# A planner's margin behind DMA loads: readers of fresh transfers placed later unless they are urgent

## The chip, the cores and the metric

The kernel runs on one core of one Trainium2 chip. The metric is device time in microseconds of one execution, as the median of several timed runs. Beside these, one execution is taken with the hardware profiler; all views of the profile come from it.

## The reference

A Mamba2-like scan over 4 sequences of 768 tokens (8 heads, head size 32, state size 16) feeds a mixture of four ReLU experts. Cut to what matters:

```python
# attention: x (4,8,768,32), a (4,8,768), B and C (4,8,768,16), float32
for c in range(nc):
    cum = np.cumsum(log_a[:, :, sl], axis=-1)
    L = np.exp(cum[:, :, :, None] - cum[:, :, None, :]) * causal
    M = np.einsum('bhin,bhjn->bhij', Cc, Bc) * L
    y[:, :, sl] = einsum(M, xc) + einsum(Cc, state) * np.exp(cum)[..., None]
    state = decay_full * state + np.sum(Bx * decay_from_j, axis=2)
x = y.transpose(0, 2, 1, 3).reshape(3072, 256)
# experts: w1 (4,256,1024), w2 (4,1024,256), domain_probs (3072,4)
p = domain_probs / (domain_probs.sum(-1, keepdims=True) + 1e-9)
for e in range(4):
    out += p[:, e:e+1] * (np.maximum(x @ w1[e], 0.0) @ w2[e])
```

## The kernel before

The 3,072 tokens are cut into 24 chunks of 128, and these into four blocks of six chunks (three pairs each; `ORDER = H, H, H, H`). The experts' hidden units are cut into 16 columns of 256. Within a block the two matrix products of the experts are done for three columns at a time with a bilinear scheme, which takes 15 block products where the plain way takes 18, at the price of sums of weights (L958), of tokens (L977) and of results (L896, L1178). One block product is `product` (L869): two matmuls of 128x128 by 128x256 in float32, four records in the profile. Sums of weights are made once, in the first block, stored to device memory (L963) and loaded again by later blocks (L955).

The attention of a chunk goes like this. `fetch` (L739) loads the chunk's tokens and B, C (`xb`, L430 to L434), the decays spread over the partitions (`ab`, L437) and those by head (`ah`, L443). `decays` makes the masks of decays with a scan on VectorE (L493, reads `ab`), the masked C on ScalarE (`mask`, L469: two multiplications of 128x128, `ctm` from `xb`), the faded B on GpSimd (`fade`, L503, reads `xb`), the decay factors (`dec`, L775, reads `ah`) and their product `cts` on GpSimd (L778). `scores` (L476) multiplies on TensorE, VectorE masks the result (L793), `outputs` (L815, L509) forms the chunk's result and `carry` (L846) the state.

None of the engines' orders after the start is written out by hand. `Plan` collects pieces of work with what each reads and writes, and with the engines that can do it and a cost in microseconds for each; some sums can go to VectorE or to GpSimd. The order of TensorE is a fixed list, `line`. `Plan.times` goes through it and gives each piece of work a time `latest`, the last start that does not make TensorE wait. `Plan.run` then walks an event clock: at each step it takes the engine that is free first, looks at its open pieces of work, finds for each when its inputs are there and its tile is free, and starts the one with the smallest `latest` among those that can start. A piece of work that isn't ready is passed over. At the end all work is issued in the order of planned starts, so each engine gets a fixed list of instructions and executes it in that order, waiting on semaphores.

All loads and stores of this part are issued from one queue, SP. The plan books a transfer with `kb` kilobytes as issue of .48 us a piece, 1.4 us, the bytes at 330 a microsecond one after another, and .7 us (L259 to L265). A reader on another engine that needs a transfer (`n.kb`) is taken as ready `MARGIN` = 2.0 us after the planned end; a reader of another engine's result as ready `HOP` = .06 us after it. `late` is how far TensorE is behind its list at that moment of the plan.

Of the kernel before, what the change touches and what calls it, by code (L numbers as in the profile page):

```python
# [18 lines left out]
HOP = 0.06  # L19
# [6 lines left out]
SOFT = 1  # L26
ROUND = 0, 4, 3, 2
RATE, MARGIN = 330.0, 2.0
AFTER = 1
HOLD = 6.0  # L30
NEAR, WORTH, FIRST = .3, 1.0, 25.0
# [45 lines left out]
class Plan:  # L77
# [105 lines left out]
    def run(self, line, at, begin):  # L183
# [19 lines left out]
        while todo:  # L203
            e = min(t, key=lambda e: t[e])
            now = t[e]
            best, soon, near = None, None, None
            late = self.late = max(0.0, t["PE"] - line[head].nominal) if head < len(line) else 0.0
            for w in waiting[e]:
                if w.start is not None or e == "PE" and w.place != head:
                    continue  # L210
                ready = max([w.ready, w.after.nominal + late if w.after else 0.0] + [
                    n.end + (MARGIN if n.kb and e != "SP" else -n.lag if n.by == e == "PE" else HOP)
                    for n in w.needs])
                if len(w.on) > 1 and e == "POOL":
                    if max(ready, now) + w.on[e] > w.latest + late + SLACK or self.backlog(
                            waiting["DVE"], now, t["DVE"], w) < (BACK if now > EASY else 99):
                        continue
                rank = w.latest
                if e == "DVE" and w.two and self.port > now + 0.05:
                    rank += YIELD  # L220
                if best is not None and ready <= now and rank >= best[0]:
                    continue
                when, homes = self.homed(
                    w, max(now, ready, self.port if e == "POOL" and w.port else 0.0))
                if when is None:
                    continue
                if when <= now + 0.02:
                    if best is None or rank < best[0]:
                        if e == "DVE" and w.two:
                            when = max(when, self.port)  # L230
                        best = rank, w, when, homes
                else:
                    if e == "DVE" and when <= now + NEAR and now < FIRST and (near is None or rank < near[0]):
                        near = rank, when
                    if soon is None or when < soon:
                        soon = when
# [16 lines left out]
            _, w, when, homes = best  # L253
# [86 lines left out]
def kernel(  # L340
# [882 lines left out]
    def leave(k, O, due):  # L1223
        for n in range(len(O)):
            o, ot = O[n], value("V")
            dve(D512, lambda e, o=o, ot=ot: nc.vector.transpose(flat(ot), flat(o)),
                reads=[o], writes=[ot])
            for c in (blocks[k].first + 2 * n, blocks[k].first + 2 * n + 1):
                dst = out[real(c) * P:real(c) * P + P].rearrange(
                    "(b i) (d a j) -> a d i b j", i=32, j=32, d=2)  # L1230
                for d in range(2):
                    for q in (0, 2):
                        def fn(e, c=c, d=d, q=q, dst=dst, ot=ot):
                            v = ot.t.rearrange("p d (b j) -> p d b j", j=32)
                            for x in (q, q + 1):
                                nc.sync.dma_start(
                                    out=dst[x, d],
                                    in_=v[32 * x:32 * x + 32, d, c % 2 * 4:c % 2 * 4 + 4])
                        dma(fn, 2, 150, reads=[ot], due=due)
# [105 lines left out]
    for u, (k, groups) in enumerate(units):  # L1345
# [20 lines left out]
        if ending is not None:  # L1366
            leave(*ending, due=lambda n=u + AFTER: ends[min(n, len(ends) - 1)])
            ending = None
# [90 lines left out]
```

## Time and profile before

| | |
|---|---|
| timed runs | 627.46, 628.15, 630.9 us; median 628.15 us |
| profiled execution, whole time | 2278.26 us |
| its span, first to last instruction | 2276.5 us |
| TensorE busy, matmul records | 2270.6 us, 3403 |
| VectorE busy | 566.9 us |
| ScalarE busy | 285.1 us |
| GpSimd busy | 132.8 us |
| moved by DMA | 99.51 MB, mean 44 GB/s |

The profiled execution is much longer than the timed runs. In the views, PE is TensorE's matmul, PEld its load of weights, DVE is VectorE, ACT is ScalarE, POOL is GpSimd and SP is the queue that issues the transfers. A line of a group has the source line, engine, operation, tiles and shapes, then busy time and mean duration in ns, then the idle time of the engine just ahead of it and what ended it. A line of waits has the engine and line that waited, what for, the total in us, how many times, and in the views of single engines the longest. A line of the timeline has the start, the duration in us, the instruction, and in brackets the idle time before it.

### The profile page before, as it was taken

What the parts mean: (1) busy time and instruction counts of PE and PEld (TensorE: products, weight loads), DVE (VectorE), ACT (ScalarE), POOL (GpSimd) and SP (SyncE); (2) the same over time, 40 slices, a digit from 0 to 9 for tenths busy, and PEclk for the clock granted to TensorE, in tenths of its full rate; (3) what the DMA queues carried; (4) which work ended last, traced back from release to release, by engine and by line L of the source; (5) the groups of instructions that cost most, each with busy time, mean ns of one, the idle gap of its engine ahead of it and who ended that gap; (6) DMA issues with size and microseconds to landing.
All of it is one profiled execution on the core that took longest, in us unless ns stands there. A gap on an engine that the chain in (4) does not pass through costs nothing.

```text
span 2276.5 us, 10010 instructions
## 1 busy us (share of the span) xinstructions
PE 2270.6 (100%) x3403; PEld 1200.0 (53%) x3403; DVE 566.9 (25%) x953; ACT 285.1 (13%) x597; POOL 132.8 (6%) x169
## 2 busy tenths in 40 slices
PE   9999999999999999999999999999999999999999
PEld 4555555555555555555555555555555555555555
DVE  3222222222222323222222231212212221212121
ACT  1000111111111111121110111101100011111100
POOL 1110101010121000000000000000000000000000
DMA  3311111111011212120011111101000211110000
GB/s 126 100 60 64 44 53 49 59 48 42 21 33 34 85 41 65 38 72 28 30 38 38 37 58 39 50 26 39 27 24 11 54 37 44 58 33 28 1 0 14
DMA packets 89203, 99.51 MB, mean 44 GB/s; under 512 B 27060, under 2 KB 62784, under 8 KB 89152
## 3 DMA queue, kind: packets, MB, share of 16 engines
q1 hardware_dynamic: 88996, 98.82, 13.9%
q8 instruction: 27, 0.44, 0.1%
q14 instruction: 24, 0.20, 0.0%
q10 hardware_dynamic: 156, 0.06, 0.0%
HBM read 82.34 MB, written 16.50 MB: 43 GB/s over the span
## 4 chain that ended last, share of the span: by engine, by line
PE 65%; ACT 0%; issue 0%
PE bank L869 64%; PE bank L509 1%; PE bank L476 1%; PE bank L815 0%; PE bank L1250 0%; ACT v L1255 0%; ACT v L830 0%; ACT A L519 0%
## 5 line engine op out<-in xcount | busy, mean ns | idle before, releaser
L869 PE MATMUL bank<-v,w 128*128 128x256 f32 x1780 | 1526.4, 1107 | 0.5 <-ACT v L830 0.5
L869 PEld LDWEIGHTS bank<-v,w 128*128 128x128 f32 x1780 | 773.0, 435 | 685.9 <-issue 671.2
L869 PE MATMUL bank<-Y,w 128*128 128x256 f32 x836 | 744.1, 1096 | 0.0
L869 PEld LDWEIGHTS bank<-Y,w 128*128 128x128 f32 x836 | 369.8, 442 | 316.4 <-issue 304.7
L904 DVE SCALAR_TENSOR_TENSOR v<-bank,gate 128x512 f32<-128x512 f32 x154 | 105.2, 689 | 681.7 <-PE bank L869 647.3
L896 DVE TENSOR_TENSOR v<-v,v 128x512 f32<-128x512 f32 x276 | 188.2, 716 | 84.0 <-ACT v L878 83.0
L896 DVE TENSOR_TENSOR v<-bank,v 128x512 f32<-128x512 f32 x76 | 52.6, 692 | 600.7 <-PE bank L869 596.1
L1127 ACT COPY v<-bank 128x512 f32<-128x512 f32 x140 | 82.1, 587 | 931.3 <-PE bank L869 931.3
L883 ACT COPY bank<-v 128x512 f32<-128x512 f32 (+1 forms) x222 | 124.4, 575 | 292.1 <-DVE v L896 210.5
L878 ACT COPY v<-bank 128x512 f32<-128x512 f32 x76 | 44.5, 586 | 493.4 <-PE bank L869 486.4
L896 POOL TENSOR_TENSOR v<-v,v 128x512 f32<-128x512 f32 x28 | 39.4, 1414 | 969.9 <-DVE v L896 553.0
L958 POOL TENSOR_TENSOR w<-w,w 128x256 f32<-128x256 f32 x48 | 36.9, 783 | 292.5 <-PE bank L869 232.3
L493 DVE TENSOR_TENSOR_SCAN LT<-ab,ident 128x512 f32<-128x512 f32 x42 | 50.5, 1218 | 0.0
L793 DVE TENSOR_TENSOR MT<-bank,LT 128x512 f32<-128x512 f32 x44 | 27.4, 683 | 69.5 <-PE bank L476 69.5
L509 PE MATMUL bank<-MT,xb 128*32 128x144 f32 (+1 forms) x384 | 44.3, 710 | 0.0
L476 PE MATMUL bank<-ctm,xb 32*128 32x256 f32 x192 | 42.1, 1055 | 1.4 <-ACT v L830 0.9
L1178 DVE TENSOR_TENSOR v<-v,v 128x256 f32<-128x256 f32 x65 | 26.1, 435 | 66.2 <-ACT v L1127 62.6
L509 PEld LDWEIGHTS bank<-MT,xb 128*32 128x32 f32 x384 | 27.6, 209 | 20.9 <-issue 17.9
L1004 DVE TENSOR_TENSOR bank<-v,bank 128x512 f32<-128x512 f32 x19 | 13.2, 696 | 86.3 <-PE bank L869 81.0
L778 POOL TENSOR_TENSOR cts<-ctm,dec 128x256 f32<-128x256 f32 x20 | 16.0, 807 | 246.8 <-DVE dec L775 177.8
L476 PEld LDWEIGHTS bank<-ctm,xb 32*128 32x128 f32 x192 | 17.4, 368 | 24.1 <-issue 20.0
L503 POOL TENSOR_TENSOR MT<-xb,LT 128x64 f32<-128x64 f32 (+1 forms) x28 | 14.1, 507 | 248.3 <-DVE LT L493 139.9
(70 smaller groups left out, 258.8 us busy)
## 6 DMA issues: line engine op xcount, KB each, us to landing
w<-w_d SPq DMA_DIRECT2D x110, 256.0 KB
w<-in_w_dram SPq DMA_DIRECT2D x88, 256.0 KB
w_d<-w SPq DMA_DIRECT2D x50, 256.0 KB
ab<-acut_d SPq DMA_DIRECT2D x21, 512.0 KB
gate<-p_d SPq DMA_DIRECT2D x18, 384.0 KB
xb<-in_xbc_dram SPq DMA_DIRECT2D x17, 192.0 KB
w<-in_w_dram SPq DMA_DIRECT2D x22, 128.0 KB
out_dram<-v SPq DMA_DIRECT2D x144, 16.0 KB
```

The source lines that it names most:

```text
L476: nc.tensor.matmul(out=views[r][:, j], lhsT=xb[j][k, OBT:OBT + P], rhs=ctm[j][k].rearrange("p t s -> p (t s)"), start=(j == 0), stop=True, ...
L493: nc.vector.tensor_tensor_scan(out=LT.rearrange("p h s -> p (h s)")[:, lo:lo + w], data0=src, data1=ident.rearrange("p h s -> p (h s)")[:, ...
L509: nc.tensor.matmul(out=y[32 * q:32 * q + 32, 0:w], lhsT=xb[:, h * D:h * D + D], rhs=MT[:, place(c, NT * q + t), 0:w], start=start, stop=Tr ...
L793: nc.vector.tensor_mul(s["MT"].t[:, js, h, 0:P], g, s["LT"].t[:, js, h])
L869: nc.tensor.matmul(out=o, lhsT=w[:, j], rhs=x if half is None else x[:, j], start=(start and j == 0), stop=(j == 1), skip_group_check=True)
L878: act(.5, lambda e: nc.scalar.copy(out=flat(v), in_=bank.t), reads=[bank], writes=[v])
L883: act(.54 if to - lo > FB else .32, lambda e: nc.scalar.copy(out=bank.t[:, lo:to], in_=flat(v)[:, lo:to]), reads=[v], writes=[bank])
L896: plan.add(engines, lambda e: (on(e).tensor_add if sign > 0 else on(e).tensor_sub)(flat(v), whole(x), whole(y)), reads=[x, y], writes=[v], ...
L904: dve(D512, lambda e: nc.vector.scalar_tensor_tensor(out=h.t, in0=whole(x).rearrange("p (j m) -> p j m", j=JJ), scalar=0.0, in1=g.t[:, 2 * ...
L958: plan.add({"POOL": .72} if due else B256, lambda e, r=r, x=x, y=y, sign=sign: (on(e).tensor_add if sign > 0 else on(e).tensor_sub)(view(r ...
L1127: act(.5, lambda e: nc.scalar.copy(out=flat(v), in_=bank.t), reads=[bank], writes=[v])
L1178: plan.add(engines, lambda e: (on(e).tensor_add if sign > 0 else on(e).tensor_sub)(o[1](), x[1](), y[1]()), reads=[v for v in vs if v is n ...
```

## The change

One line of `Plan.run` changes, and two constants come in. A reader of a transfer that is not on SP is still taken as ready 2.0 us after the planned end of the transfer while the plan's clock is below `SURE` = 100, or when its `latest` (moved by `late`) is less than 8 us away. Otherwise it is taken as ready `LEEWAY` = 6.0 us after the planned end. TensorE's list is not touched. As the planner picks by what is ready, a reader that is held back gives its place to other work, and what follows in the plan can fall differently: the order of instructions on each engine, the tile that a value gets, and for some sums the engine.

```diff
 RATE, MARGIN = 330.0, 2.0
+LEEWAY, SURE = 6.0, 100.0
 AFTER = 1
...
                 ready = max([w.ready, w.after.nominal + late if w.after else 0.0] + [
-                    n.end + (MARGIN if n.kb and e != "SP" else -n.lag if n.by == e == "PE" else HOP)
+                    n.end + ((MARGIN if now < SURE or w.latest + late < now + 8 else LEEWAY) if n.kb and e != "SP" else -n.lag if n.by == e == "PE" else HOP)
                     for n in w.needs])
```

Lines of the changed kernel after L28 are numbered one higher than before; the texts here use the numbers of the kernel before unless they show a line of the other.

## The prediction

> **What bounds the kernel now.** I read the busy table first, then the chain of waits, the groups of PE, the waits by engine, and last the timeline and the windows around single transfers. The busy table and the two lines of the chain:
>
> ```profile
> PE 2270.6 (100%) x3403; PEld 1200.0 (53%) x3403; DVE 566.9 (25%) x953; ACT 285.1 (13%) x597; POOL 132.8 (6%) x169
> ...
> PE 65%; ACT 0%; issue 0%
> PE bank L869 64%; PE bank L509 1%; PE bank L476 1%; PE bank L815 0%; PE bank L1250 0%; ACT v L1255 0%; ACT v L830 0%; ACT A L519 0%
> ...
> L869 PE MATMUL bank<-v,w 128*128 128x256 f32 x1780 | 1526.4, 1107 | 0.5 <-ACT v L830 0.5
> ...
> L869 PE MATMUL bank<-Y,w 128*128 128x256 f32 x836 | 744.1, 1096 | 0.0
> ```
>
> PE is never without work: before 2,616 matmul records it stood idle 0.5 us. But this execution took 2278.26 us (span 2276.5, 1.76 around it) and the timed runs 628.15, so it is 3.6 times as long as what I must forecast. The timeline of PE near the end shows why: weight loads follow each other at 0.84 us.
>
> ```profile
> 2267.22 0.47 PEld L869 LDWEIGHTS bank<-v,w 128*128 128x128 f32 x1 [0.38 <-issue]
> 2268.06 0.48 PEld L869 LDWEIGHTS bank<-v,w 128*128 128x128 f32 x1 [0.37 <-issue]
> 2268.90 0.48 PEld L869 LDWEIGHTS bank<-v,w 128*128 128x128 f32 x1 [0.36 <-issue]
> ```
>
> 2,616 x 0.84 = 2197 us of the 2270.6. At that pace the timed median is impossible: 2197 alone exceeds it. The code books .863 us for one `product`, which is four such records, so 0.216 each; 2,616 x 0.216 = 565 us does fit into 628.15. I therefore take PE as 0.84 / 0.216 = 3.9 times slow in the trace and all other engines as they are (a 128x512 add on DVE took 0.716 us). What follows from it for the reader: waits that PE's slowness covers in the trace may be open in the timed runs. Other work in the timed runs: the remaining 73 us of PE are 19 us when divided by 3.9, the traced end after the last copy (2273.30 + 0.37 to 2276.5) is 2.8 us, and what lies around the span 1.8. That leaves 628 - 565 - 19 - 3 - 2 = 39 us for the start and every wait of PE together. The first product stands at 25.93 us in the trace, behind a start that PE's slowness lengthens too; with 13 to 26 us for that start, PE's waits come to 13 to 26 us in the whole kernel.
>
> **What the Trainium skill says.** On "TensorE: Matmul & The Clock Gate", in the caveats of "Part 1: The HAM clock gate", the clock has been seen stuck at a quarter. The factor 3.9 agrees with that, while the trace's own clock column reads 1.00; no run shown decides between them. The same page, "Architectural detail", has ACT and DVE as strict first-in-first-out queues, so a reader whose data is late holds up all behind it. The trace agrees on POOL, below: it stood 55.56 us before one reader of `xb`. "DMA: Bandwidth & Descriptors", "Rules for kernel authors", advises to issue early and wait late, which is what the edit does. "SBUF — State Buffer", "SBUF: two separate sides", says that DVE with two SBUF inputs and GpSimd take turns on an exclusive port pair; the two DVE sums `w<-w` at 907 ns, where the 42 of form `w<-w,w` take 442, look like such a turn.
>
> **The readers of transfers.** Waits that DMA ended, from the waits of ACT and of POOL:
>
> ```profile
> ACT ctm L469 <- DMA xb<-in_xbc_dram: 1.3, 2, 0.8
> ...
> POOL MT L503 <- DMA xb<-in_xbc_dram: 55.6, 1, 55.6
> ```
>
> ACT's wait on DMA is small beside the 931.3 us for which its copies at L1127 waited for PE, and the timeline of ACT puts both ACT waits (0.47 and 0.81 us) at 149 and 151 us, before the planner's time 100 from which the edit acts (the first moved mask is the one at 337.24). The POOL wait gives the landing time. The timelines of SP and POOL:
>
> ```profile
> 964.21 0.33 SPq L430 DMA_DIRECT2D xb<-in_xbc_dram  x1
> 964.64 0.85 SPq L432 DMA_DIRECT2D xb<-in_xbc_dram  x2
> ...
> 966.79 0.41 POOL L503 TENSOR_TENSOR MT<-xb,LT 128x128 f32<-128x128 f32 x1 [55.56 <-DMA xb<-in_xbc_dram]
> ```
>
> From the first issue to the start of the reader: 966.79 - 964.21 = 2.58 us, semaphore included. The planner's formula for the same three pieces is 3 x .48 for issue, 1.4, 107 KB / 330 for the last piece, .7: 3.86 us. So it is already 1.3 us late, and `MARGIN` adds 2.0: the reader stands 3.3 us behind its data. A 512 KB `ab` load, issued at 514.99 and alone, moved its bytes in the windows from 515.5 to 518.0 (49, 287, 377, 279, 57 GB/s), where the formula says .48 + 1.4 + 1.55 + .7 = 4.1 us after issue. For a crowded queue: six issues from 427.74 to 434.79 ended in bytes until 437, some 2.2 us after the last issue, and the formula ends 2.5 us after it (437.3). The margin is thus whole there too. At the timed pace the same bytes go in 3.6 times less time: 99.51 MB / 628 us = 158 GB/s, 42% of the 377 seen. From 171 to 1400 us the traced rates are 39 to 55 GB/s, 140 to 200 at the timed pace, while the first 57 us have 126 GB/s. The stretch in which transfers could come later than the plan is the one that `SURE` leaves out.
>
> **The change part by part,** by the order of instructions in the two built programs.
>
> 1. *PE:* all 681 pieces of work in the same order, only bank and tile numbers differ. 0 us.
> 2. *ACT masks (L469, two of 0.39 us a pair):* 12 of 24 pairs come after planner time 100, two of these are urgent and keep the margin, ten are moved behind 2 to 7 pieces of ACT work. 0 us of busy time. Cover: the scores (L476) that read them, and `cts` (L778) on POOL, which feeds the outputs after the scores. The traced distance from mask to scores is 77 us at the least (1364.62 to 1441.76), about 20 at the timed pace, and the move is some 4 us. If that cover went, the scores would be late next, and with them the products behind them on PE.
> 3. *Waits removed:* in the trace none after planner time 100 on ACT, so 0; at the timed pace between 0 and ten times the mean of the two traced waits, 10 x 0.64 = 6.4 us. I take 0.5 us, near the traced end, because the readers already stand 3.3 us behind their data.
> 4. *Sums and adds that change engine in the ripple:* nine 512-wide adds go from POOL to DVE and eight back, two sums L958 against one, two L1178 against none. DVE + 0.72 + 0.44 + 2 x 0.44 = +2.0 us of 567; POOL - 1.41 - 0.78 - 2 x 0.88 = -4.0. Neither bounds anything. On the path: 0 as taken, between -5.6 and +5.6, since each of the eight adds that move to POOL is 1.414 - 0.716 = 0.70 us slower there, and the nine the other way gain as much.
> 5. *DVE order:* scans and state transposes move by up to some 80 places, the far ones forward, into gaps; the add of 0.45 us or scan of 1.22 us that then stands before an urgent one costs at most its own length. It is inside the bounds of 4.
> 6. *SP order:* 413 rows both times; stores of weight sums (0.42 us of issue each) fall back by 2 to 5 places behind loads, one `ah` load comes 15 earlier, two sets of eight output stores swap. Nothing waits for the stores within the block. 0; the waits of SP's queue end in PE (L955 waited 678.7 us for it), so loads remain tied to PE. POOL issues no transfers.
>
> Sum: -0.5 us on a median of 628.15: **627.6**. On the profiled execution itself the sum is 0 of 2278.26, as every wait concerned lies under PE.
>
> **The rivals.** A measurement of this kernel can tell about 0.5% (3.1 us) from no change.
>
> *A, the fresh readers do block at the timed pace.* Ten mask pairs wait 0.64 us each and ACT's copies to and from PSUM behind them (L883, L878) reach PE late: -6.4 us, 621.8. It takes five of them for 0.5%. For it: strict queues, and PE slow enough in the trace to hide this. Against it: 3.3 us of margin measured.
>
> *B, slower: an add moved to POOL becomes the last thing that a product waits for.* Eight adds at +0.70 us make +5.6, 633.7; from five on the path it decides. For it: PE waited for DVE's adds 21 times in the trace (8.1 us in all, PEld), so they are the nearest to the path, and a POOL add holds the port. Against it: the planner gives POOL only what it expects to be early, and no PE wait in the trace ends in a POOL add.
>
> *C, the change doesn't do what it says where it matters.* The readers nearest to PE, the two urgent mask pairs and their scans, keep `MARGIN`; only readers with 8 us to spare are moved. Then nothing: 628.15.
>
> **How the numbers follow.** My forecast and C give the same answer within 0.5%: 0.65 together. A has 0.17, B 0.18; the room for A is capped by waits of 13 to 26 us in all, most of which have nothing to do with fresh transfers. Own range of the likeliest case: 625.0 to 631.3. For 8 in 10 it has to take in the greater part of A and of B: 623.5 to 632.5.
>
> **What would show it.** In the changed kernel's profile: masks of ten pairs later among ACT's copies; ACT still without a wait on DMA after 337 us; PE's order and idle time unchanged. A is right if PE's waits on ACT copies shrink by microseconds; B if PE's waits on POOL or DVE adds grow. A profile with PE at the timed pace would show waits that this one hides; I would be wrong if it has ACT or POOL idle before L469, L503 or L958 for more than 3 us in sum, ended by DMA, with PE waiting behind them.

## The result, and the profile after

The changed kernel takes 625.75 us (median of 18 runs, 623.83 to 626.94); the kernel before, timed beside it, 627.71 us (18 runs, 626.7 to 630.9). The ratio is 0.9961, 95% interval 0.995 to 0.9972, so the change saves about 2.4 us of 628; the two medians differ by 1.96 us. The gain is inside the 0.5% that the prediction called no change, and the median is 1.85 us below its 627.6; the interval excludes a ratio of 1.

TensorE ran at its timed pace in the profiled execution of the changed kernel (626.94 us around a span of 625.2). For a like-for-like view the kernel before was profiled once more (first experiment); that execution had the timed pace too: 627.95 us, span 626.2. From here on "before" is that execution. The page of the changed kernel, busy table, chain and groups:

```profile
PE 613.9 (98%) x3403; PEld 521.5 (83%) x3403; DVE 562.4 (90%) x957; ACT 281.9 (45%) x597; POOL 147.6 (24%) x165
...
PE 47%; DVE 1%; DMA 1%; issue 0%; ACT 0%
...
L870 PE MATMUL bank<-v,w 128*128 128x256 f32 x1780 | 423.1, 380 | 2.0 <-DVE v L905 0.9
...
L870 PE MATMUL bank<-Y,w 128*128 128x256 f32 x836 | 215.3, 380 | 2.7 <-DVE v L897 1.5
```

The same lines of the kernel before:

```profile
PE 614.4 (98%) x3403; PEld 521.6 (83%) x3403; DVE 564.7 (90%) x953; ACT 281.5 (45%) x597; POOL 154.3 (25%) x169
...
L869 PE MATMUL bank<-v,w 128*128 128x256 f32 x1780 | 423.2, 380 | 2.1 <-ACT bank L883 1.6
...
L869 PE MATMUL bank<-Y,w 128*128 128x256 f32 x836 | 215.5, 380 | 3.5 <-DVE v L896 1.8
```

Two things are to be seen. TensorE is idle for 626.2 - 614.4 = 11.8 us before and 625.2 - 613.9 = 11.3 us after, so shortening waits alone can hardly win more than that. And VectorE is at 90%, not at the 25% of the stretched execution. In the windows of the kernel before (window, its length, then busy us and count of PE, PEld, DVE, ACT, POOL, then the granted clock, the DMA share and GB/s) it has next to no slack from 100 to 300 us. Time in which GpSimd holds it up counts as busy here:

```profile
100.00:200.00 100.00, 98.64 (x514) 83.96 (x513) 99.06 (x158) 52.64 (x109) 56.43 (x55) 1.00 0.49 159
200.00:300.00 100.00, 97.73 (x589) 82.75 (x588) 98.42 (x164) 52.07 (x115) 26.39 (x27) 1.00 0.64 201
```

TensorE has the same 3,403 records in the same order in both kernels, so the start of each can be set against the start of its twin. The table gives by how many us the changed kernel is ahead (-) or behind (+) of the one before over each stretch, for the profile above and for a second one of the changed kernel (623.84 us, tenth experiment):

| stretch of the kernel before, us | profile of 626.94 us | profile of 623.84 us |
|---|---|---|
| 0 to 22 | +0.90 | -0.30 |
| 22 to 117 | -0.20 | -0.69 |
| 117 to 142 | -0.85 | -0.85 |
| 142 to 205 | +0.97 | -0.42 |
| 205 to 229 | -0.77 | -0.76 |
| 229 to 307 | +0.06 | +0.03 |
| 307 to 340 | -0.99 | -1.00 |
| 340 to the end | -0.13 | -0.12 |
| sum | -1.01 | -4.11 |

The sums agree with the times of these executions (626.94 and 623.84 against 627.95). Three places gain in both profiles: near 135, near 225 and near 317 us. The opening, where the two plans are the same, differs by 1.2 us from run to run and is not the change. The row of 22 to 117 us is within such differences too: two kernels of the experiments whose plan is that of before for most of this row (the masks alone, two places) lie at -0.58 and -0.25 there.

The last of these places shows one thing that happens. The kernel before, timeline:

```profile
312.11 2.94 POOL L896 TENSOR_TENSOR v<-v,v 128x512 f32<-128x512 f32 x2 [1.23 <-DVE v L896]
...
312.56 3.04 DVE L896 TENSOR_TENSOR v<-v,v 128x512 f32<-128x512 f32 x2
...
315.52 2.47 DVE L793 TENSOR_TENSOR MT<-bank,LT 128x512 f32<-128x512 f32 x4
316.29 0.59 ACT L883 COPY bank<-v 128x512 f32<-128x512 f32 x1 [10.27 <-DVE MT L793]
...
316.93 1.13 PE L869 MATMUL bank<-v,w 128*128 128x256 f32 x4 [1.42 <-ACT bank L883]
```

Two VectorE sums take 3.04 us while two GpSimd sums run beside them; a pair without company takes 1.28 us (below). The masking of the scores (L793) starts that much later, the copy into PSUM waits for it, and TensorE stops: 1.80 us between two starts where 0.22 is normal. The changed kernel, same place:

```profile
308.30 5.07 POOL L897 TENSOR_TENSOR v<-v,v 128x512 f32<-128x512 f32 x2 [15.66 <-DVE v L897]
...
311.07 2.85 DVE L897 TENSOR_TENSOR v<-v,v 128x512 f32<-128x512 f32 x2
...
313.84 0.68 DVE L905 SCALAR_TENSOR_TENSOR v<-bank,gate 128x512 f32<-128x512 f32 x1
...
314.57 2.86 PE L870 MATMUL bank<-v,w 128*128 128x256 f32 x12 [0.87 <-DVE v L905]
```

The sums meet again, but 1.5 us earlier and ahead of another piece. TensorE waits 0.87 us for the gating L905, and the stop at 317 us is gone: the gap before that gating is 0.94 us longer than in the kernel before, the stop and the records just behind it are 1.93 us shorter, and that makes the -0.99 of the table.

The place near 225 us is of another kind. The kernel before, VectorE and TensorE:

```profile
219.62 1.21 DVE L493 TENSOR_TENSOR_SCAN LT<-ab,ident 128x512 f32<-128x512 f32 x1
...
224.79 0.66 DVE L904 SCALAR_TENSOR_TENSOR v<-bank,gate 128x512 f32<-128x512 f32 x1
...
225.50 1.13 PE L869 MATMUL bank<-Y,w 128*128 128x256 f32 x4 [0.71 <-DVE v L904]
```

The changed kernel:

```profile
224.22 0.66 DVE L905 SCALAR_TENSOR_TENSOR v<-bank,gate 128x512 f32<-128x512 f32 x1
...
226.42 1.13 PE L870 MATMUL bank<-v,w 128*128 128x256 f32 x4 [0.36 <-ACT bank L884]
```

Between 217 us and that gating VectorE runs four scans before and three after the change; the scan at 219.62 us is the one that is gone from there. No VectorE piece in this stretch is held up by GpSimd in the kernel before. The stop of 1.08 us between starts is gone, and one of 0.73 us stands one product later. In the profiles of the experiments the stop is there, at 1.08 or 1.09 us, in each kernel with the four scans, and the same gap is never above 0.42 us in those with three. Which scans stand there was not changed by itself.

Waits that DMA ended, in the timelines of ACT and POOL after 100 us; the kernel before:

```profile
106.26 0.69 ACT L469 ACTIVATE ctm<-xb,tmask 128x128 f32<-128x128 f32 x2 [0.25 <-DMA xb<-in_xbc_dram]
...
243.00 2.12 POOL L896 TENSOR_TENSOR v<-v,v 128x512 f32<-128x512 f32 x1 [1.29 <-DMA ab<-acut_d]
275.97 0.41 POOL L503 TENSOR_TENSOR MT<-xb,LT 128x128 f32<-128x128 f32 x1 [12.89 <-DMA xb<-in_xbc_dram]
282.60 0.76 POOL L778 TENSOR_TENSOR cts<-ctm,dec 128x256 f32<-128x256 f32 x1 [0.37 <-DMA xb<-in_xbc_dram]
```

The changed kernel:

```profile
130.15 0.73 POOL L959 TENSOR_TENSOR w<-w,w 128x256 f32<-128x256 f32 x1 [6.30 <-DMA w<-in_w_dram]
134.77 0.72 POOL L959 TENSOR_TENSOR w<-w,w 128x256 f32<-128x256 f32 x1 [3.89 <-DMA xb<-in_xbc_dram]
142.62 2.04 POOL L959 TENSOR_TENSOR w<-w,w 128x256 f32<-128x256 f32 x2 [0.23 <-DMA w<-in_w_dram]
276.81 0.69 POOL L504 TENSOR_TENSOR MT<-xb,LT 128x128 f32<-128x128 f32 x1 [16.97 <-DMA xb<-in_xbc_dram]
```

Of ScalarE's waits on DMA, 0.25 us lay after 100 us, so there was next to nothing to remove. GpSimd's went from 14.6 to 27.4 us, up and not down. No row of the waits of TensorE's matmuls names GpSimd or DMA in either kernel; its weight loads waited 0.9 and 0.7 us for transfers and 0.9 and 1.4 us for GpSimd.

### The profile page after: what moved, and what is told of

The parts are those of the page before. It is cut to its first block, busy times and chain, and to the rows that moved or that the text cites. A ratio compares the mean times of both kernels' runs of the same rounds, so it can differ in the third digit from the quotient of the medians.

```text
span 625.2 us, 10016 instructions
## 1 busy us (share of the span) xinstructions
PE 613.9 (98%) x3403; PEld 521.5 (83%) x3403; DVE 562.4 (90%) x957; ACT 281.9 (45%) x597; POOL 147.6 (24%) x165
## 5 line engine op out<-in xcount | busy, mean ns | idle before, releaser
L870 PE MATMUL bank<-v,w 128*128 128x256 f32 x1780 | 423.1, 380 | 2.0 <-DVE v L905 0.9
L870 PEld LDWEIGHTS bank<-v,w 128*128 128x128 f32 x1780 | 336.3, 190 | 53.5 <-issue 3.5
L870 PE MATMUL bank<-Y,w 128*128 128x256 f32 x836 | 215.3, 380 | 2.7 <-DVE v L897 1.5
L870 PEld LDWEIGHTS bank<-Y,w 128*128 128x128 f32 x836 | 158.1, 190 | 27.1 <-DVE v L897 2.7
L905 DVE SCALAR_TENSOR_TENSOR v<-bank,gate 128x512 f32<-128x512 f32 x154 | 103.6, 681 | 15.9 <-PE bank L870 15.3
L959 POOL TENSOR_TENSOR w<-w,w 128x256 f32<-128x256 f32 x47 | 46.5, 1004 | 40.4 <-PE bank L870 21.5
L1179 DVE TENSOR_TENSOR v<-v,v 128x256 f32<-128x256 f32 x67 | 25.7, 417 | 6.7 <-ACT v L1128 6.6
L1179 POOL TENSOR_TENSOR v<-v,v 128x256 f32<-128x256 f32 x15 | 14.5, 980 | 60.9 <-DVE v L1179 42.0
L905 DVE SCALAR_TENSOR_TENSOR v<-v,gate 128x512 f32<-128x512 f32 x38 | 28.2, 741 | 0.5
L897 DVE TENSOR_TENSOR v<-v,bank 128x512 f32<-128x512 f32 x38 | 25.7, 677 | 0.0
L470 ACT ACTIVATE ctm<-xb,tmask 128x128 f32<-128x128 f32 x48 | 16.2, 395 | 14.3 <-DMA xb<-in_xbc_dram 14.2
L959 DVE TENSOR_TENSOR w<-w,w 128x256 f32<-128x256 f32 x43 | 16.3, 425 | 0.0
```

The source lines that it names most:

```text
L470: nc.scalar.mul(ctm[:, t], xb[:, OCT:OCT + P], tmask[:, t:t + 1])
L870: nc.tensor.matmul(out=o, lhsT=w[:, j], rhs=x if half is None else x[:, j], start=(start and j == 0), stop=(j == 1), skip_group_check=True)
L897: plan.add(engines, lambda e: (on(e).tensor_add if sign > 0 else on(e).tensor_sub)(flat(v), whole(x), whole(y)), reads=[x, y], writes=[v], ...
L905: dve(D512, lambda e: nc.vector.scalar_tensor_tensor(out=h.t, in0=whole(x).rearrange("p (j m) -> p j m", j=JJ), scalar=0.0, in1=g.t[:, 2 * ...
L959: plan.add({"POOL": .72} if due else B256, lambda e, r=r, x=x, y=y, sign=sign: (on(e).tensor_add if sign > 0 else on(e).tensor_sub)(view(r ...
L1179: plan.add(engines, lambda e: (on(e).tensor_add if sign > 0 else on(e).tensor_sub)(o[1](), x[1](), y[1]()), reads=[v for v in vs if v is n ...
```

## The experiments

Three theories. **M:** the masks on ScalarE waited for their data and held up the copies behind them (rival A of the prediction). **R**, wider: what counts is that readers, on whatever engine, stand further behind their transfers. **L:** the moved readers are only the trigger; the order of VectorE and GpSimd falls differently, and the gain is the net of places where a VectorE piece that TensorE is about to need comes earlier or later, above all because a GpSimd operation holds it up.

**The kernel before, once more** (no edit; label e1_before_again).

> The kernel before, unchanged, for a profile at the timed pace (the one shown had a TensorE four times slow). Theory M (fresh masks block ScalarE): ScalarE's waits on DMA before the masks (L469) after the plan's time 100 come to 3 us or more above those of the changed kernel, and TensorE's idle time is 2 to 3 us above the 11.3 us of the changed kernel, behind ScalarE copies. Theory R (the ripple of other moves gives the gain, the masks none): these waits on DMA are the same within 1 us or smaller than in the changed kernel, and TensorE's extra idle time lies behind VectorE or GpSimd sums.

One run, 627.95 us, profiled at the timed pace. What it showed is above. The stops of TensorE that it made visible end in VectorE sums (L896), gatings (L904), mask products (L793) and in ScalarE's copies behind these.

**The masks alone** (e2_masks_only). The plan of the kernel before; ten pairs of masks (L469) and four `cts` (L778) are issued where the changed kernel has them. `moved` gives the planned start for the number of a piece of work; its one line is broken here.

```diff
+    moved = {910: 105.381, 901: 111.781, 1139: 134.864, 1148: 143.265, 1567: 284.883,
+             1576: 285.653, 1811: 290.384, 1803: 295.303, 1928: 384.500, 1936: 385.469,
+             1569: 285.990, 1578: 291.410, 1930: 385.435, 1938: 386.239}
+    for w in done:
+        w.start = moved.get(w.number, w.start)
+    done.sort(key=lambda w: w.start)
     for w in done:
         w.fn(w.by)
```

> The kernel before with its own plan; only the ten mask pairs (L469) are issued where the changed kernel has them, and the four cts products (L778) that directly follow behind them; every other order, engine and tile is that of before. Theory M (the masks behind fresh loads blocked ScalarE): faster by 2 us or more, ratio 0.997 or less. Theory R (the ripple through the other orders gives the gain): ratio 0.999 to 1.001, and TensorE's stalls of before near 135 us (0.8 us) and 317 us (1.8 us) are still there.

Ratio 1.0002 (0.9993 to 1.0012). The stop near 317 us is there as before:

```profile
311.99 2.93 POOL L896 TENSOR_TENSOR v<-v,v 128x512 f32<-128x512 f32 x2 [1.23 <-DVE v L896]
312.43 3.04 DVE L896 TENSOR_TENSOR v<-v,v 128x512 f32<-128x512 f32 x2
...
316.80 1.13 PE L869 MATMUL bank<-v,w 128*128 128x256 f32 x4 [1.44 <-ACT bank L883]
```

The small one near 135 us was absent in this profile. One of the ten mask pairs had stood there (129.07 us, now 134.00), so this run cannot tell whether its move did that or a small shift between the engines: GpSimd's adds began 0.20 us ahead of the VectorE pair in the kernel before, which then took 2.21 us, and 0.08 us behind it here, where it took 1.27.

**The masks put back** (e3_masks_back): the changed kernel with the ten pairs where the kernel before has them, same form of edit.

> The changed kernel with its own plan; only the ten mask pairs are issued where the kernel before has them. Theory M: the gain is gone, ratio 0.999 to 1.001. Theory R: the gain stays, ratio 0.995 to 0.9975.

0.9963 (0.9948 to 0.9978): the whole gain stays. With the run before it, M falls as the cause of the gain in both directions.

**The edit for GpSimd's readers only, and for ScalarE's only** (e4_gpsimd_only, e5_scalar_only).

```diff
-(MARGIN if now < SURE or w.latest + late < now + 8 else LEEWAY)
+(MARGIN if now < SURE or e != "POOL" or w.latest + late < now + 8 else LEEWAY)   # the other: e != "ACT"
```

> The edit in the planner for readers on GpSimd alone (weight sums L958, fade L503); ScalarE's and VectorE's readers keep 2.0 us. Theory M: nothing, ratio 0.999 to 1.001. Theory R says that it depends on where GpSimd's sums come to stand beside VectorE's: if the held weight sums near 131 us are what matters, most of the gain, 0.996 to 0.998.

> The edit in the planner for readers on ScalarE alone (the masks). Theory M: the whole gain, ratio 0.995 to 0.9975. Theory R: whatever the ripple of this variant gives, between 0.996 and 1.003, most likely within 0.001 of 1; ScalarE's waits on DMA after 100 us stay under 1 us either way.

0.9969 (0.996 to 0.9978) and 1.0033 (1.0015 to 1.005). The half for GpSimd is nearly as good as the whole; the half for ScalarE is slower than the kernel before. In the first, the pair of sums near 313 us ran alone:

```profile
313.03 1.27 DVE L897 TENSOR_TENSOR v<-v,v 128x512 f32<-128x512 f32 x2
```

TensorE gains 1.94 us on the kernel before between 307 and 340 us there, after losing 2.7 us between 142 and 229 at stops of its own. In the second the pair took 2.04 us, the stop near 317 became one near 315 (2.21 us between starts), and another grew from 0.95 to 2.15 us at 247 us. This execution took 627.95 us, as long as the one of the kernel before, so it does not show the loss. That lies in five of the eleven executions (630.56 to 631.86 us), whose mean granted clock is 0.996 or 0.997; the other six, at 0.999 or 1.0, have a median of 628.27, 0.07% above the kernel before. Of the five there is no profile. The gain of the half for GpSimd fits L, and R as well; the loss of the half for ScalarE fits L, while M and R have no reason for one.

**Two sums moved, nothing else** (e6_two_sums_moved). This tests L without any of the change: in the plan of before, the two GpSimd sums of 312.11 us go to VectorE, behind the mask products.

```diff
+    moved = {1350: ("DVE", 317.95), 1345: ("DVE", 318.0)}
+    for w in done:
+        w.by, w.start = moved.get(w.number, (w.by, w.start))
+    done.sort(key=lambda w: w.start)
     for w in done:
```

> The plan of the kernel before, unchanged but for two v<-v,v sums of L896 (128x512): they leave GpSimd's queue, where they ran at 312.11 us for 2.94 us beside two DVE sums of 3.04 us, and are issued on VectorE behind the four mask products L793 that follow. Nothing of the change under study is in it, no reader of a transfer moves. Theory L (sums of the two engines hold each other up, and TensorE stops where a late VectorE piece ends in its input): the two DVE sums at 312.6 us fall from 3.04 to about 1.3 us, the L793 products start about 1.8 us earlier, and the 1.8 us gap of TensorE at 316.93 us falls to 0.4 or less; about -1.4 us in all, ratio 0.9975 to 0.9985. The rival R (what counts is the place of the readers of transfers, not the sums): ratio 1.000 within 0.001 and the gap stays. If VectorE has no room for 1.3 us more behind the products, the gap only moves and the ratio is 1.000 too, with the gap at another place.

0.9979 (0.997 to 0.9988), as L forecast. The profile of this kernel runs some 4 us late by then: at 59 us, where its plan is that of before, ScalarE's masks waited for `xb` (10.79 and 1.37 us) and a copy behind them for TensorE came late. So the block that M means does occur, in one execution and in the stretch that `SURE` leaves out. The place itself reads:

```profile
316.50 1.28 DVE L896 TENSOR_TENSOR v<-v,v 128x512 f32<-128x512 f32 x2
...
317.46 1.78 PE L869 MATMUL bank<-v,w 128*128 128x256 f32 x7
317.70 1.88 DVE L793 TENSOR_TENSOR MT<-bank,LT 128x512 f32<-128x512 f32 x3
```

The pair is back at 1.28 us and the 1.80 us gap at 0.22; 1.76 us are won from 307 to 340 us, and nothing is lost later.

**Two places** (e7_two_places): besides, three adds L958 leave GpSimd for VectorE at 135 us (`493`, `494`, `495` in `moved`).

> As the run with two sums moved, and besides the three L958 adds (128x256) that GpSimd runs at 131.72 us for 2.99 us, beside two DVE sums of 2.21 us, are issued on VectorE behind the L904 gatings that follow. Theory L: the DVE sums at 131.9 us fall to 1.3 us, TensorE's gap at 135.37 us (0.76 between starts, 0.22 without a stall) goes, -0.5 us, so that this kernel is 0.4 to 0.6 us faster than the one with the first place alone: ratio 0.9965 to 0.9975, which is as far as the whole change goes (0.996) with five instructions moved. Against it: the three adds cost VectorE 1.0 us where it is busy all the time, so the 0.5 us may be lost again at the next gap (161.69 us, 0.53). Rival R: 1.000.

0.9981 (0.9971 to 0.9991), no better than one place. The stop at 135 us went (-0.55), as L has it, but the next, at 161.8 us, grew from 0.53 to 1.40 us between starts; that the 1.0 us of adds put on a full VectorE came out there is the likeliest reading, as these adds are all that sets the two kernels apart. The expectation named this way to fail; its main figure was wrong.

**Other sizes of LEEWAY**, 4 and 9 in place of 6 (e8_leeway_4, e9_leeway_9), one number each.

> The changed kernel with LEEWAY = 4.0 in place of 6.0, nothing else. If the gain is that of readers standing further behind their data (R), 4 us lies between the 2.05 us of before and 6 us: a ratio between 0.9961 and 1, about 0.997 to 0.999, and the gap at 316.9 us smaller than 1.8 us. If the gain is the chance outcome of another interleaving of the sums (L), the ratio is not ordered by LEEWAY: anything from 0.993 to 1.004, with gaps of 0.5 to 2 us at places of its own, each behind a VectorE sum or product that ran beside GpSimd sums.

> The changed kernel with LEEWAY = 9.0 in place of 6.0, nothing else. R: at least as fast as at 6 us, ratio 0.994 to 0.9965. L: not ordered by LEEWAY, 0.993 to 1.004, gaps at places of its own.

1.0081 (1.0064 to 1.0098) at 4 and 1.0026 (1.0017 to 1.0035) at 9, against 0.9961 at 6. R wanted an order in these numbers; there is none. Part of both losses is the clock. At 9 us 13 of 22 executions have a mean granted clock of 0.996 or 0.997 and a median of 630.12 us, the other nine 628.0, 0.07% above the kernel before; at 4 us all four have 0.994 to 0.997. The last section shows the clock in the profiles. The order is missing without it too: 6 us gains, and 9 us at the higher clock does not. The loss at 4 us reads so in its timeline:

```profile
145.44 2.94 DVE L897 TENSOR_TENSOR v<-v,v 128x512 f32<-128x512 f32 x3
...
145.58 4.26 POOL L959 TENSOR_TENSOR w<-w,w 128x256 f32<-128x256 f32 x4
...
149.18 1.21 DVE L897 TENSOR_TENSOR v<-v,v 128x512 f32<-128x512 f32 x1
150.31 1.21 DVE L494 TENSOR_TENSOR_SCAN LT<-ab,ident 128x512 f32<-128x512 f32 x1
...
153.97 2.07 PE L870 MATMUL bank<-Y,w 128*128 128x256 f32 x4 [3.38 <-DVE v L905]
```

Sums beside GpSimd's adds, a scan ahead of the urgent sums, and TensorE stands for 3.4 us; about 3 us more go at half pace behind it. At 9 us the pair of 317 us is back, in front of a gating:

```profile
312.83 2.94 POOL L897 TENSOR_TENSOR v<-v,v 128x512 f32<-128x512 f32 x2 [1.23 <-DVE v L897]
313.27 3.04 DVE L897 TENSOR_TENSOR v<-v,v 128x512 f32<-128x512 f32 x2
...
316.97 1.65 PE L870 MATMUL bank<-v,w 128*128 128x256 f32 x3 [2.50 <-DVE v L905]
```

**The changed kernel again, and with its own sums moved** (e10_after_again, no edit; e11_after_sums_moved: `1349` and `1345` from GpSimd, and `1350` on VectorE, behind the mask products).

> The changed kernel unchanged, for a second profile and more times: its profiled execution was the longest of its runs (626.94 against a median of 625.75). Every theory: ratio 0.995 to 0.997, and a median near 625.7 us. Theory L: the gap of TensorE at 316.9 us is absent again, that of 0.9 us at 314.6 us is there again behind the two GpSimd sums of 5.07 us; the opening up to 22 us, where the profiled run was already 0.9 us behind the kernel before, varies between runs.

> The changed kernel with the measure of the run with two sums moved: the two L897 sums (128x512) that GpSimd runs at 308.3 us for 5.07 us beside a VectorE pair of 2.85 us, and one VectorE sum of the same kind ahead of the L794 mask products, are issued on VectorE behind those products. Theory L: the VectorE pair falls from 2.85 to about 1.3 us, the gating L905 at 313.84 us ends 1.5 us earlier, and TensorE's gap of 0.87 us at 314.57 us goes: -0.7 to -1.0 us against the changed kernel, ratio to the kernel before 0.9940 to 0.9955, median 624.4 to 625.2 us. Rival R (place of the readers): no change against the changed kernel, 0.9961. Against it: VectorE gets 1.3 us more to do and, busy nearly all the time until 339 us, may pass the delay on to a later gap.

The first repeats the result: 625.6 us, 0.9965 (0.9952 to 0.9977), with the same 0.87 us stop. Its profile, 3.1 us shorter than the first, has the stop at 189.7 us (0.91 between starts) missing: ahead of it a GpSimd triple (L1179) had lain over a VectorE sum and a gating (1.02 and 1.21 us); in the second profile VectorE reached the sum 0.7 us earlier beside TensorE and was nearly done with it when the triple began, and the two took 0.68 us each. The second is the fastest of all: median 623.99 us, 0.9947 (0.9926 to 0.9969).

```profile
309.42 1.29 DVE L897 TENSOR_TENSOR v<-v,v 128x512 f32<-128x512 f32 x2
...
310.62 0.69 DVE L905 SCALAR_TENSOR_TENSOR v<-bank,gate 128x512 f32<-128x512 f32 x1
```

The pair falls from 2.85 to 1.29 us, and the gap of 1.25 us between starts becomes 0.30, -0.94 us against the changed kernel. It beats the kernel before; its interval overlaps that of the changed kernel, and against that one only the removed stop is shown.

## Why the prediction was right, and where it was wrong

*The range and the sign* held: 625.75 lies in 623.5 to 632.5, and the change is worth less than 0.5%. What was right in the reasoning is that ScalarE's readers hardly wait after planner time 100, and that TensorE does not wait behind those of GpSimd, which do. The sign was luck: it came from step 3 alone, and those waits were not there. The size, -0.5 against -2.4, was off by a factor of nearly five, because the gain came from a term that was set at nothing.

*What bounds the kernel:* TensorE's pace was read rightly (records 0.216 us apart in both new profiles), but its waits were overestimated: start and waits were put at 39 us, and all idle time of TensorE is 11.8. The sum went wrong in the other records: 2,616 x 0.84 is too much, as some of these records follow at 0.68 us and the mean in that trace is 0.82, so more than 73 us were left for the rest; at the timed pace the rest takes 45 us from start to start, not 19, and with 45 the same sum leaves 13 us. The clock column that reads 1.00 for that execution is no evidence: its page has no row for the granted clock, as the pages of all the other executions have. The failing step beside it is the reading of the other engines. VectorE's 566.9 us were taken from the stretched execution with its share of 25%; divided by the 628 us of the timed runs the same number is 90%. "Neither bounds anything" in step 4 is where the prediction broke: on an engine that is nearly full for 200 us, a late piece stays late.

*Step 1,* TensorE's order: right, 0. *Step 2,* masks at 0 us: right, shown by moving them alone (1.0002) and back (0.9963). But the steps name no other moved reader, and the edit for GpSimd's readers alone, the weight sums (L958) and fades (L503), brings nearly the whole gain (0.9969). *Step 3,* 0.5 us for waits removed: wrong in kind. ScalarE had 0.25 us of such waits after 100 us, and the masks are not what gained. The sign that the prediction named for being wrong came in its first half only: in the kernel before, GpSimd stood 12.89 us before a fade for its data, but TensorE did not wait behind it. In the reading of the crowded queue, eight issues and not six stand from 427.74 to 434.79; the end of the bytes is read rightly.

*Steps 4 and 5,* taken as 0 within -5.6 to +5.6: this is the mis-sized term; every part of the 2.4 us that a run or a trace has located lies in it. The bound was wide enough, its price was not the right one. It counted 0.70 us for a sum that is slower on GpSimd, while GpSimd's own time doesn't matter; what costs is that a VectorE pair beside two GpSimd sums takes 3.04 us in place of 1.28. The Trainium skill's "SBUF — State Buffer", section "SBUF: two separate sides", which the prediction cited for two slow sums, says that a VectorE operation with two SBUF inputs and a GpSimd operation exclude each other for the whole of an instruction; the 3.04 us and their return to 1.28 us in the run with two sums moved agree with it. The prediction quoted the rule and then priced the swaps without it. `Plan.run` itself keeps such pieces apart on its clock (`port`), and they met all the same on the chip, so the plan's times are no proof against it. Step 5 named the case near 225 us, a scan ahead of an urgent piece, and the scan went the good way there.

*Step 6,* SP's order at 0: no wait of TensorE's matmuls in the changed kernel ends in a transfer, and its weight loads waited 0.7 us for some, against 0.9 before; no run takes this order apart from the rest.

*The rivals.* A falls with M. TensorE's waits for ScalarE's copies into PSUM did shrink, from 1.9 to 0.8 us, but 1.42 of them was the copy at 317 us, which itself waited for VectorE. B named the right pair of engines and the wrong place: no stop of TensorE ends in a GpSimd sum, and those that were isolated lie behind VectorE pieces that one has held up. A loss, as B forecast it, did come with other settings: the edit for ScalarE alone and LEEWAY at 4 and 9 are slower by 0.26 to 0.81%, in part through the clock. That 6 us fell on the good side is luck of the plan rather than merit of the margin. C, no effect at all, is excluded by the interval, barely in size.

*Open:* How the 2.4 us divide over the places. Only the stop at 317 us and the one at 314.6 us were isolated (about 1.6 and 0.9 us). The one near 135 us went when its adds were moved, but also in the profile of the masks alone; the one near 225 us is read from traces, and stops of 0.3 to 0.9 us come and go between executions of one kernel. Not run by themselves were the margin for VectorE's readers (the scans) and the changed tile and bank numbers.

## What to carry to other kernels

When a planner's rule is changed, its direct effect may be nothing while the reshuffled order is worth a few us either way: undo the direct effect alone, and try the neighbouring values of the constant, before believing the reason. When a profiled execution is stretched by one engine, divide the other engines' busy times by the timed span before calling any of them free. Where VectorE is full, look for GpSimd sums that lie over a VectorE piece that TensorE will need next, and move those few.

## What the runs showed of the hardware

Two VectorE sums of 128x512 with both inputs in SBUF take 1.28 us alone and 3.04 us beside two GpSimd sums; a VectorE gating with both inputs in SBUF took 1.21 us for 0.68 in the same way. GpSimd suffers too: a pair took 5.07 us beside a row of VectorE sums, where one sum alone took 1.27.

A long stop of TensorE can cost more than its length. After it had been idle for 2.5 us (LEEWAY at 9), 2.7 us (the stop at 59 us) and 3.4 us (LEEWAY at 4), its records followed each other at 0.43 us for 6, 8 and 14 records before returning to 0.22. After stops of up to 2.2 us between starts they did not. With LEEWAY at 4 this added 3.0 us to a stop of 3.5. The granted clock shows it too. In these three traces the times between its changes are whole multiples of 3.41 us (310.6 and 3.4 with LEEWAY at 9, 58.0 and 3.4 around the stop at 59 us, 146.8 and 6.8 with LEEWAY at 4). The windows of LEEWAY at 9 around its stop, in the form of the windows above:

```profile
313.10:316.50 3.40, 1.37 (x18) 0.72 (x16) 3.40 (x4) 0.59 (x1) 2.67 (x2) 1.00 0.28 82
316.50:319.90 3.40, 2.93 (x7) 2.39 (x8) 3.40 (x7) 1.41 (x3) 0.00 (x0) 0.50 0.00 0
319.90:323.30 3.40, 3.40 (x17) 2.99 (x17) 2.87 (x9) 2.44 (x6) 0.72 (x1) 1.00 0.40 119
```

The clock fell to half after stretches of this grid in which TensorE was busy for 1.37, 0.68 and 0.69 us of 3.40; after 1.63 us (the stop at 247 us with the edit for ScalarE alone) it stayed full. So how a stop lies on the grid may decide whether an execution gets the lower clock; that would fit executions of one kernel with and without it, but it was not tested. The Trainium skill, "TensorE: Matmul & The Clock Gate", "Part 1: The HAM clock gate", gives half pace after an idle window of about 3.4 us, and calls this window free-running; the halving and the 3.41 us agree, and here it already came after an idle time of 2.5 us, 2.0 of them within one such stretch.
